# Zero products on TensorE near the start, and projection operands at half a 64-byte line

## The chip, the cores and the metric

The kernel runs on one core of a Trainium2 chip. The metric is the device time of one execution in microseconds. Before the change it is 289.07 us, the median of 3 runs (288.51 to 289.23).

## The reference

Inputs are float32. Attention has 2 batches, 8 heads, 768 positions and 64 elements a head; a query sees the first 8 keys and the 96 keys that end at itself, with a linear bias by distance and head. Its output goes through two gated networks. What is computed, cut to what matters:

```
scores = q @ k.T / sqrt(64) - slope[h] * dist         # outside the window: -1e9
x  = (softmax(scores) @ v) as [2, 768, 512]
g1 = sigmoid(causal depthwise conv of x, 5 taps)
x  = (g1 * (x @ w_val)) @ w_out                       # 512 -> 512 -> 512
h  = relu(x @ w_in)                                   # 512 -> 1024
g2 = sigmoid(depthwise conv of h, 3 taps)
out = (h * g2) @ w_out2                               # 1024 -> 512
```

## The kernel before, in words

A tile is 128 partitions high. Attention works on 12 tiles of 128 queries (2 batches of 6). For each, PE makes the scores against this tile's keys and those of the tile before (`scores`, L461), DVE adds the bias and takes the maximum (`least`, L472), ACT takes the exponential (L477), DVE divides by the sum (L498), PE transposes (L522) and multiplies with the values (L540). These products are plain f32; each leaves two records in the trace. The keys of tile 0 are loaded ahead of all else into a part of `c.x` that is still free (L835, L836); tile 1 is the first that uses keys loaded in the main part (`load`, L434).

The weights come as 64-bit floats and are turned into f32 by ACT, POOL and DVE (`to_f32`, L252). `w_out` and `w_in` are multiplied with each other once (`weights`, L319, f32, into two banks called f), so that the two layers between the gates are one. Every operand of the later products is split in a high and a low part of type fp32r (`split_ops`), and a product is three matmuls (`mm3`, L243 to L245): high by high, high by low, low by high. The 768 positions go in two chunks of 400 and 368 columns a batch, four in all. For each chunk `values` multiplies with `w_val` (moving operand `gx`), `hidden` with the joined weights `Wh`, `Wl` (moving operand `gg`), DVE convolves and gates, and `project` multiplies the result `g2` (loaded as stationary operand) with `w_out2` (moving operand, 512 columns, called wo2 here and lying in four tiles named w8). In the last chunk, the last of its three groups of rows is split into two halves of 256 columns, and the very last half goes out by DVE (L802) and a DMA.

SBUF tiles lie in pools one behind the other, in steps of 32 bytes: `const` (x, ident, Wh, Wl, wv), `w8`, `wst` (raw, m: staging of weights), `sg` (z, gx, gg, h, z2), and then `at` (attention's tiles) or, when attention is done, `late` (g2, o) in the same place; `small` lies at the other end. In the kernel before, every pool begins on a 64-byte line; inside `at`, the tile `st` of 96 bytes in three buffers leaves v and pts at half a line, and inside `sg` every second h tile is at half a line. PSUM has eight banks: four s, one t, one x, two f.

The order of the work around the change: the first part of the program is written out by hand (L833 to L845): DMAs, position and mask tiles, and the load of two numbers into registers of each engine (`values_load_multi_w_load_instructions`, L841), on which a branch between two forms of the kernel hangs (L938). All the rest is laid out by a planner (`Plan`): each piece of work has an engine, a cost in microseconds, the buffers that it holds and the names that it reads and writes; the planner lays the pieces on a model of the engines, and the order so found is the order in which each engine gets its instructions. A piece with `mode="s"` is drawn to others of its mode on PE.

Of the kernel before, what the change touches and what calls it, by code (L numbers as in the profile page):

```python
# [9 lines left out]
F32 = mybir.dt.float32  # L10
# [5 lines left out]
PSUM = bass.MemoryType.PSUM  # L16

P = 128
# [208 lines left out]
def dma_us(kb):  # L227
    return max(0.4, kb / 385.0)
# [118 lines left out]
        parts_unit(c, c.w_out2, a, lambda z, a=a, two=two: two[z].t[:, a % 4, :], two, ("wo2", a))  # L347


def scratch(c):  # L350

    x = [c.x[:, d, XP:] for d in range(NC1)]
    c.rel, c.w, c.d = (x[d][:, 0:WIN] for d in range(3))
    c.key, c.far, c.d0 = (x[d][:, 4 * P : 5 * P] for d in range(3))


def positions(c):

    nc = c.nc
    nc.gpsimd.iota(c.rel, pattern=[[-1, WIN]], base=P, channel_multiplier=1, allow_small_or_imprecise_dtypes=True)  # L360
    nc.gpsimd.iota(c.key, pattern=[[1, P]], base=0, channel_multiplier=0, allow_small_or_imprecise_dtypes=True)
    nc.gpsimd.affine_select(
        out=c.rel, in_=c.rel, compare_op=ALU.is_ge, fill=BIG, base=P, pattern=[[-1, WIN]], channel_multiplier=1
    )


def first_mask(c):

    nc = c.nc
    lf = c.small.tile([P, 2], F32, name="lf")  # L370
    nc.vector.tensor_copy(lf, c.li[:, :, 0])
    c.ng, c.nl = ng, nl = lf[:, 0:1], lf[:, 1:2]
    rel, w = c.rel[:, P:], c.w[:, P:]
    nc.vector.tensor_scalar(c.far, c.key, ng, BIG, ALU.is_ge, ALU.mult)
    nc.vector.scalar_tensor_tensor(w, rel, nl, c.far, ALU.is_ge, ALU.mult)
    nc.vector.scalar_tensor_tensor(c.d0, rel, nl, w, ALU.min, ALU.add)
# [32 lines left out]
def fast_attention(c, ap):  # L409

    nc, ident, pl = c.nc, c.ident, c.plan
# [9 lines left out]
    kq, vs = {}, {}  # L421
# [7 lines left out]
    def load(t):  # L429
        b, i = tiles[t]  # L430
        if t == 0:
            return
        kq[t], vs[t] = kqr.new(), vr.new()
        pl.add("SP", dma_us(512), lambda: nc.sync.dma_start(kq[t].t, c.kq[b, i]), [kq[t]], [], [("kq", t)], delay=LANDING)  # L434
        src = c.v[b, i * P : (i + 1) * P].rearrange("s h d -> s (h d)")
        pl.add(
            "SP", dma_us(256), lambda: nc.sync.dma_start(vs[t].t.rearrange("p a h d -> p (a h d)"), src),
            [vs[t]], [], [("v", t)], delay=LANDING,
        )

    def held(d, ts):
        return [d[t] for t in ts if t in d]

    for t in range(nt):
# [3 lines left out]
        js = [t - 1, t] if i else [t]  # L448
        nk = len(js) * P
        st, p = sts.new(), {}  # L450
        load(t)
        for half in range(2):
            s = [c.ring["s"].new() for z in range(2)]

            def scores(half=half, s=s, js=js, t0=t):
# [5 lines left out]
                            nc.tensor.matmul(out, keys(t0, pr, 1)[hs], keys(j, pr, 0)[hs], start=True, stop=True)  # L461

            pl.add(
                "PE", 0.43 * len(js), scores, s + held(kq, js), [("kq", j) for j in js], [("s", t, half)], mode="s"
            )
            for h in range(4 * half, 4 * half + 4):
                p[h] = pr_.new()
# [345 lines left out]
def attention_gated_mlps(ctx, tc, kq, v, nn, w_val, conv_w, w_out, w_in2, w_out2, out):  # L813
    nc = tc.nc
    c = Ctx()
# [4 lines left out]
    c.const = ctx.enter_context(tc.tile_pool(name="const", bufs=1))  # L820
    w8 = ctx.enter_context(tc.tile_pool(name="w8", bufs=1))
    c.wst = ctx.enter_context(tc.tile_pool(name="wst", bufs=1))
    sg = ctx.enter_context(tc.tile_pool(name="sg", bufs=1))
    c.small = ctx.enter_context(tc.tile_pool(name="small", bufs=1, side="right"))
    c.x = c.const.tile([P, NC1, XW], F32, name="x")
# [7 lines left out]
    with tc.manual_schedule():  # L833
        nc.sync.dma_start(c.li.rearrange("p n t -> p (n t)"), c.nn.to_broadcast([P, 4]))
        nc.scalar.dma_start(k0[:, 0:2], kq[0, 0, :, 0:2])  # L835
        nc.sync.dma_start(k0[:, 2:4], kq[0, 0, :, 2:4])  # L836
        nc.scalar.dma_start(v0, v[0, 0:P].rearrange("s (a h) d -> s a h d", a=4))
        scratch(c)
        positions(c)
        nc.vector.memset(one, 0.0)  # L840
        _, (glo, ghi, llo, lhi) = nc.values_load_multi_w_load_instructions(c.nn)  # L841
        nc.scalar.activation(one, one, AF.Exp)
        nc.gpsimd.memset(c.x[:, :, 0:XP], 0.0)
        make_identity(nc, c.ident)
        first_mask(c)  # L845
# [9 lines left out]
    def arm(fast):  # L855
        with ExitStack() as es:
# [4 lines left out]
            pl = c.plan = Plan()  # L861
            ap = pools.enter_context(tc.tile_pool(name="at", bufs=1)) if fast else None
            late = {}

            def late_pool():
                if not late:
                    pools.close()
                    late["p"] = pools.enter_context(tc.tile_pool(name="late", bufs=1, reuse_waits="tile"))
                return late["p"]

            def all_keys(b):
# [16 lines left out]
            c.ring["h"] = sb(here, "h", [P, CW + 2], F32, HBUFS)  # L888
            c.ring["z2"] = sb(here, "z2", [P, CH], F32, Z2BUFS)
            c.ring["g2"] = sb(late_pool, "g2", [P, 2, CH], F32R, 8)  # L890
            c.ring["o"] = sb(late_pool, "o", [P, DM], F32, 2)
            c.raws = sb(lambda: c.wst, "raw", [P, 512, 2], I32, RAWS)
            c.ms = sb(lambda: c.wst, "m", [P, 512], F32, MBUFS)
# [5 lines left out]
            if fast:  # L899
                masks(c, ap)  # L900
                attention = fast_attention(c, ap)
                next(attention)
                n0 = len(pl.work)
# [78 lines left out]
```

## Time and profile before

| | |
|---|---|
| median of 3 runs | 289.07 us |
| profiled execution | 288.96 us |
| its span | 287.2 us |
| PE busy | 269.2 us (94%), 1832 instructions |
| DVE busy | 238.6 us (83%) |
| ACT busy | 192.6 us (67%) |
| POOL busy | 68.5 us (24%) |
| HBM read, written | 22.59 MB, 3.15 MB |

The span runs from the first to the last instruction of the profiled execution. PE is the matmul engine (TensorE), PEld its loads of stationary operands, DVE VectorE, ACT ScalarE, POOL GpSimd, SPq the queue that issues most DMAs. Busy time is that in which an engine has an instruction under way; matmuls overlap each other, so that the duration of one is more than the time between two starts. `s<-w,g` are the projection's matmuls, `f<-gg,Wh` and the like the hidden layer's, `s<-kq` the attention's scores.

### The profile page before, as it was taken

The page shows a single profiled execution, that of the slowest core. Times are in us where ns is not written, and L with a number is a line of the kernel's source. Part 1 is how long each engine was busy: PE and PEld are TensorE (multiplying, and loading weights), DVE is VectorE, ACT ScalarE, POOL GpSimd, SP SyncE. Part 2 cuts the span into 40 slices and gives each one's busy share as a digit, 9 for nine tenths or more (in the row PEclk, how much of TensorE's full clock was granted, in tenths as well). Part 3 has the DMA queues.
Part 4 walks back from the last instruction along what each step waited for, and adds up shares of the span by engine and source line. Part 5 has one row for each costly group of instructions (what it writes and reads, how often), then busy time and mean ns, then how long its engine had stood idle before and what let it go on. Part 6 is the DMA issues. An engine that isn't in the chain of part 4 may idle for free.

```text
span 287.2 us, 5402 instructions
## 1 busy us (share of the span) xinstructions
PE 269.2 (94%) x1832; PEld 228.0 (79%) x1832; DVE 238.6 (83%) x637; ACT 192.6 (67%) x486; POOL 68.5 (24%) x160
## 2 busy tenths in 40 slices
PE   2687899899999999999999999999999999999993
PEld 2565666565447999999999999988999988899882
DVE  3999999999999999999899999999986654357600
ACT  2899998988568989988778544875355354454510
POOL 4422223522111120212353512360612000003000
PEclk9999999999999999999999999999999999999999
DMA  4984668637406301004510000010000011000112
GB/s 132 362 312 168 188 216 266 237 102 266 149 2 219 102 19 49 10 2 155 181 40 0 2 0 1 1 39 37 38 2 0 0 73 39 37 0 2 40 73 84
DMA packets 10277, 26.18 MB, mean 91 GB/s; under 512 B 1408, under 2 KB 2688, under 8 KB 10240
## 3 DMA queue, kind: packets, MB, share of 16 engines
q1 hardware_dynamic: 9440, 25.22, 26.3%
q10 hardware_dynamic: 800, 0.52, 0.6%
q8 instruction: 16, 0.26, 0.4%
q14 instruction: 21, 0.17, 0.2%
HBM read 22.59 MB, written 3.15 MB: 90 GB/s over the span
## 4 chain that ended last, share of the span: by engine, by line
PE 72%; DVE 20%; issue 3%; DMA 2%; ACT 1%; POOL 1%; SPq 0%; DVEq 0%; POOLq 0%
PE s L244 8%; PE s L245 8%; PE s L243 8%; PE f L243 7%; PE f L245 7%; PE f L244 7%; DVE p L472 5%; DVE p L498 4%; PE s L461 4%; PE x L540 4%; PE t L522 4%; DVE raw L269 3%; PE t L243 2%; PE x L245 2%; PE t L245 2%
## 5 line engine op out<-in xcount | busy, mean ns | idle before, releaser
L652 DVE SCALAR_TENSOR_TENSOR z<-h,cw,z 128x384 f32<-128x384 f32 x64 | 40.6, 643 | 12.6 <-ACT z L647 10.9
L477 ACT ACTIVATE p<-p,st 128x256 f32<-128x256 f32 (+1 forms) x96 | 46.0, 482 | 5.8 <-DVE st L472 5.5
L654 ACT ACTIVATE z<-z 128x384 f32<-128x384 f32 (+2 forms) x48 | 25.0, 523 | 26.7 <-DVE z L652 26.4
L244 PE MATMUL s<-w,g 128*128 128x512 f32 (+1 forms) x104 | 39.2, 377 | 0.0
L245 PE MATMUL s<-w,g 128*128 128x512 f32 (+1 forms) x104 | 39.2, 377 | 0.0
L243 PE MATMUL s<-w,g 128*128 128x512 f32 (+1 forms) x104 | 39.1, 376 | 0.0
L652 DVE SCALAR_TENSOR_TENSOR z<-x,cw,z 128x400 f32<-128x400 f32 (+1 forms) x64 | 38.4, 628 | 0.1
L522 PE MATMUL t<-ident,p 128*128 128x128 f32 x176 | 28.6, 281 | 4.7 <-ACT pts L526 4.7
L498 DVE TENSOR_SCALAR p<-p,st 128x256 f32<-128x256 f32 (+1 forms) x96 | 31.1, 368 | 0.7
L522 PEld LDWEIGHTS t<-ident,p 128*128 128x128 f32 x176 | 19.9, 140 | 14.6 <-ACT pts L526 8.5
L472 DVE CUSTOM_DVE_ANT_0 p<-s,B 128x256 f32<-128x256 f32 x80 | 30.7, 417 | 0.4 <-PE t L522 0.4
L319 PE MATMUL f<-w,w 128*128 128x512 f32 x64 | 30.1, 601 | 0.7 <-DVE Wl L236 0.6
L526 ACT ACTIVATE pts<-t 128x512 f32<-128x512 f32 (+1 forms) x48 | 26.5, 553 | 2.5 <-PE t L522 2.1
L243 PE MATMUL f<-gg,Wh 128*128 128x400 f32 (+1 forms) x80 | 27.7, 346 | 0.0
L245 PE MATMUL f<-gg,Wl 128*128 128x400 f32 (+1 forms) x80 | 27.0, 338 | 0.0
L244 PE MATMUL f<-gg,Wh 128*128 128x400 f32 (+1 forms) x80 | 27.0, 338 | 0.0
L461 PE MATMUL s<-kq 64*128 64x128 f32 x320 | 25.0, 291 | 0.5 <-DVE st L472 0.5
L461 PEld LDWEIGHTS s<-kq 64*128 64x128 f32 x320 | 21.0, 194 | 5.5 <-issue 3.2
L264 POOL TENSOR_SCALAR raw<-raw 128x512 f32<-128x512 f32 x24 | 17.7, 739 | 27.2 <-ACT m L262 21.6
L648 POOL TENSOR_SCALAR z<-h,cw 128x384 f32<-128x384 f32 x12 | 11.4, 947 | 49.1 <-DVE z L652 31.0
L245 PEld LDWEIGHTS s<-w,g 128*128 128x128 f32 x104 | 19.5, 188 | 3.8
L236 DVE TENSOR_TENSOR g<-z,g 128x384 fp32r<-128x384 f32 x32 | 17.4, 550 | 5.9 <-ACT g L234 5.9
(114 smaller groups left out, 606.4 us busy)
## 6 DMA issues: line engine op xcount, KB each, us to landing
raw<-in_moe_w_out_dram SPq DMA_DIRECT2D x12, 512.0 KB, 3.4
kq<-in_kq_dram SPq DMA_DIRECT2D x11, 512.0 KB, 5.1
raw<-in_moe_w_in_dram SPq DMA_DIRECT2D x8, 512.0 KB, 4.4
v<-in_v_dram SPq DMA_DIRECT2D x11, 256.0 KB, 3.9
out_dram<-o SPq DMA_DIRECT2D x11, 256.0 KB, 2.0
raw<-in_moe_w_val_dram SPq DMA_DIRECT2D x4, 512.0 KB, 4.0
v<-in_v_dram SPq DMA_DIRECT2D x8, 64.0 KB, 2.7
x<-in_kq_dram ACTq DMA_DIRECT2D x1, 256.0 KB, 4.1
```

Of the source, the lines that this page charges most:

```text
L243: nc.tensor.matmul(out, lh, rh, start=first, stop=False)
L244: nc.tensor.matmul(out, lh, rl, start=False, stop=False)
L245: nc.tensor.matmul(out, ll, rh, start=False, stop=last)
L319: nc.tensor.matmul(ps.t, big["wot"].t.bitcast(F32)[:, e, cs], big[wi].t.bitcast(F32)[:, e, :], start=e == 0, stop=e == 3)
L461: nc.tensor.matmul(out, keys(t0, pr, 1)[hs], keys(j, pr, 0)[hs], start=True, stop=True)
L472: nc.vector.tensor_tensor_reduce(w.t[:, :nk], sc, bias, -QKSCALE, 3.0e38, ALU.add, ALU.min, st.t[:, 0, h : h + 1])
L477: nc.scalar.activation(w.t[:, :nk], w.t[:, :nk], AF.Exp, bias=st.t[:, 0, h : h + 1], scale=-1.0, accum_out=st.t[:, 1, h : h + 1],)
L498: nc.vector.tensor_scalar(w.t[:, :nk], w.t[:, :nk], st.t[:, 2, h : h + 1], None, ALU.mult)
L522: nc.tensor.transpose(o[:, z, n, :], p[2 * pr + z].t[:, n * P : (n + 1) * P], ident)
L526: nc.scalar.activation(w.t[:, :, :nw, :], o[:, :, :nw, :], AF.Copy)
L652: nc.vector.scalar_tensor_tensor(z(), src(k), w()[:, k : k + 1], z(), ALU.mult, ALU.add)
L654: pl.add("ACT", act_us(n), lambda: nc.scalar.activation(z(), z(), AF.Tanh, scale=0.5), bufs, [], [token])
```

## The change

It does three things. A new function `idle` issues f32 products of zeros, with both operands read from one constant. Three of them, of 512, 512 and 256 columns, stand ahead of the register load in a PSUM pool of their own, closed at once. Two more, of 512 columns, are a piece of planned work on PE with cost 1.72 us and one f bank; it reads the names of tile 0's scores, and tile 1's scores read its name, so that it stands between them. Last, an unused tile of 32 bytes is put at the head of the pools `w8`, `wst` and `late`.

```diff
--- before.py
+++ after.py
@@ -347,6 +347,13 @@
         parts_unit(c, c.w_out2, a, lambda z, a=a, two=two: two[z].t[:, a % 4, :], two, ("wo2", a))
 
 
+def idle(c, out, widths):
+
+    for n in widths:
+        zeros = [c.nc.const_aps.tensor(0.0, [P, w], F32) for w in (P, n)]
+        c.nc.tensor.matmul(out[:, :n], *zeros, start=True, stop=True)
+
+
 def scratch(c):
 
     x = [c.x[:, d, XP:] for d in range(NC1)]
@@ -449,6 +456,9 @@
         nk = len(js) * P
         st, p = sts.new(), {}
         load(t)
+        if t == 1:
+            rest = c.ring["f"].new()
+            pl.add("PE", 1.72, lambda rest=rest: idle(c, rest.t, [512, 512]), [rest], [("s", 0, half) for half in range(2)], ["idle"])
         for half in range(2):
             s = [c.ring["s"].new() for z in range(2)]
 
@@ -461,7 +471,7 @@
                             nc.tensor.matmul(out, keys(t0, pr, 1)[hs], keys(j, pr, 0)[hs], start=True, stop=True)
 
             pl.add(
-                "PE", 0.43 * len(js), scores, s + held(kq, js), [("kq", j) for j in js], [("s", t, half)], mode="s"
+                "PE", 0.43 * len(js), scores, s + held(kq, js), [("kq", j) for j in js] + ["idle"] * (t == 1), [("s", t, half)], mode="s"
             )
             for h in range(4 * half, 4 * half + 4):
                 p[h] = pr_.new()
@@ -820,6 +830,8 @@
     c.const = ctx.enter_context(tc.tile_pool(name="const", bufs=1))
     w8 = ctx.enter_context(tc.tile_pool(name="w8", bufs=1))
     c.wst = ctx.enter_context(tc.tile_pool(name="wst", bufs=1))
+    for pool in (w8, c.wst):
+        pool.tile([P, 8], F32, name="half_line")
     sg = ctx.enter_context(tc.tile_pool(name="sg", bufs=1))
     c.small = ctx.enter_context(tc.tile_pool(name="small", bufs=1, side="right"))
     c.x = c.const.tile([P, NC1, XW], F32, name="x")
@@ -835,6 +847,8 @@
         nc.scalar.dma_start(k0[:, 0:2], kq[0, 0, :, 0:2])
         nc.sync.dma_start(k0[:, 2:4], kq[0, 0, :, 2:4])
         nc.scalar.dma_start(v0, v[0, 0:P].rearrange("s (a h) d -> s a h d", a=4))
+        with tc.tile_pool(name="pw", bufs=1, space=PSUM) as pw:
+            idle(c, pw.tile([P, 512], F32, name="idle"), [512, 512, 256])
         scratch(c)
         positions(c)
         nc.vector.memset(one, 0.0)
@@ -866,6 +880,7 @@
                 if not late:
                     pools.close()
                     late["p"] = pools.enter_context(tc.tile_pool(name="late", bufs=1, reuse_waits="tile"))
+                    late["p"].tile([P, 8], F32, name="half_line")
                 return late["p"]
 
             def all_keys(b):
```

## Rows read from the trace of the kernel before

**Rows 1.** the page, busy us, share of the span and instructions of each engine
```profile
PE 269.2 (94%) x1832; PEld 228.0 (79%) x1832; DVE 238.6 (83%) x637; ACT 192.6 (67%) x486; POOL 68.5 (24%) x160
```

**Rows 2.** stages: from:to, length, busy us of each engine, PEclk, DMA share, GB/s
```profile
0.00:4.90 4.90, 0.00 (x0) 0.00 (x0) 0.58 (x4) 0.23 (x1) 1.34 (x9) 1.00 0.39 125
...
9.05:12.87 3.82, 3.79 (x33) 3.59 (x34) 3.75 (x20) 3.26 (x13) 1.62 (x5) 1.00 1.03 370
12.87:30.00 17.13, 13.95 (x158) 10.68 (x159) 16.23 (x66) 16.23 (x53) 4.94 (x12) 1.00 0.69 242
30.00:80.75 50.75, 48.57 (x364) 30.32 (x364) 50.00 (x166) 43.09 (x127) 15.48 (x28) 1.00 0.62 197
...
142.80:282.70 139.90, 139.42 (x734) 127.43 (x732) 104.68 (x193) 74.65 (x151) 30.04 (x66) 1.00 0.07 25
```

**Rows 3.** chain of waits: start us, us, what
```profile
9.10 3.77 PE s L461 x32
```

**Rows 4.** timeline: start us, us, engine, line, tiles, count [idle before, releaser]
```profile
0.81 0.06 DVE L840 MEMSET one<- 128x1 f32 x1 [0.81 <-PEq L956]
...
4.97 2.08 PE L461 MATMUL s<-x 64*128 64x128 f32 x16 [4.97 <-DMA x<-in_kq_dram]
...
6.03 0.72 DVE L385 TENSOR_SCALAR b<-x 128x128 f32<-128x128 f32 x3 [0.45 <-DVE x L376]
...
6.66 0.28 DVE L472 CUSTOM_DVE_ANT_0 p<-s,b 128x128 f32<-128x128 f32 x1
...
9.08 0.80 PE L461 MATMUL s<-x,kq 64*128 64x128 f32 x4 [2.03 <-DVE x L401]
...
11.59 0.42 DVE L472 CUSTOM_DVE_ANT_0 p<-s,B 128x256 f32<-128x256 f32 x1
...
13.28 0.42 DVE L472 CUSTOM_DVE_ANT_0 p<-s,B 128x256 f32<-128x256 f32 x1 [0.38 <-PE t L522]
...
14.08 1.16 PE L461 MATMUL s<-kq 64*128 64x128 f32 x16
```

**Rows 5.** groups by line and form, PE: count, busy us, mean ns, idle
```profile
L244 PE MATMUL s<-w,g 128*128 128x512 f32 x88 | 34.8, 396 | 0.0
...
L319 PE MATMUL f<-w,w 128*128 128x512 f32 x64 | 30.1, 601 | 0.7 <-DVE Wl L236 0.6
...
L243 PE MATMUL f<-gg,Wh 128*128 128x368 f32 x32 | 10.6, 331 | 0.0
L244 PE MATMUL f<-gg,Wh 128*128 128x368 f32 x32 | 10.5, 329 | 0.0
...
L244 PE MATMUL s<-w,g 128*128 128x256 f32 x16 | 4.4, 276 | 0.0
...
L461 PE MATMUL s<-x 64*128 64x128 f32 x16 | 2.1, 435 | 5.0 <-DMA x<-in_kq_dram 5.0
```

**Rows 6.** timeline of PE, ten records of L319
```profile
69.70 4.46 PE L319 MATMUL f<-w,w 128*128 128x512 f32 x10
```

**Rows 7.** the projection's matmuls alone in their stretch, busy us of PE
```profile
142.80:282.70 139.90, 71.30 (x312) 1.00 0.07 25
```

**Rows 8.** timeline of PE: projection, then hidden layer, from start to start
```profile
250.46 0.39 PE L243 MATMUL s<-w,g 128*128 128x512 f32 x1
250.69 0.39 PE L244 MATMUL s<-w,g 128*128 128x512 f32 x1
...
251.16 0.39 PE L243 MATMUL s<-w,g 128*128 128x512 f32 x1
...
253.25 0.33 PE L243 MATMUL x<-gg,Wh 128*128 128x368 f32 x1
...
255.27 0.33 PE L243 MATMUL f<-gg,Wh 128*128 128x368 f32 x1
```

**Rows 9.** timeline of PE, the attention's products L540
```profile
129.00 1.97 PE L540 MATMUL x<-pts,v 128*64 128x128 f32 x32
```

**Rows 10.** line L652 on DVE: duration ns min/median/max, first and last start
```profile
L652 DVE SCALAR_TENSOR_TENSOR z<-h,cw,z x64: 601/617/999, 125.4 to 269.8; 128x384 f32<-128x384 f32 x64
```

## The prediction

> **What bounds the kernel now.** I read the busy times first [rows 1]: PE 94%, DVE 83%. A mean over stages says little, so the stages come next [rows 2]. There the reader sees three kernels in one. Until 9.05 us everything waits for loads and masks. From there to 80.75 us DVE is the full engine (3.75 of 3.82 us, 50.00 of 50.75). From 142.8 to 282.7 us it is PE (139.42 of 139.90), while DVE has room (104.68). Third, the chain of waits [rows 3] gives the order: in its early part PE's scores of the second tile, 3.77 us from 9.10, between stretches of DVE; later PE all along, and at the end DVE's last copy and the output's DMA. Fourth, the timeline tells PE's pace inside the stages, from start to start, since the duration of one matmul is a latency that overlaps the next.
>
> **The register load and the first zeros.** The first scores start at 4.97 and sixteen records take 2.08 us; at 14.08 sixteen of the same size take 1.16 us [rows 4], the second group being of another tile. So PE runs at 1.2 GHz at first and at 2.4 GHz by 14.08, although the windows print a granted clock of 1.00 from the start [rows 2]. After the first scores PE idles 2.03 us and then works from 9.08, still slowly.
>
> The change puts three f32 products of 512, 512 and 256 columns ahead of the register load. Price: an f32 product leaves two records (L319's 32 products leave 64 [rows 5]); ten such records take 4.46 us, the last of them 0.60, so (4.46 - 0.60)/9 = 0.43 us each at 2.4 GHz [rows 6]. 512 columns are 0.86 us, 1280 columns 2.15 us, and at half clock 4.3 us. PE has nothing else until 4.9 us (x0 in rows 2). Starting near 0.8 us, where DVE starts its first instruction [rows 4], the zeros end near 5.1 us, 0.1 us after the scores' present start. Cover: DVE makes masks from 6.03 to 6.75 and reads its first scores at 6.66 [rows 4]; the first half of the scores, (2.08 - 0.43)/2 after their start and a latency of 0.43 [rows 5], is there at 6.2, or 6.3 with the delay. So the delay costs nothing, and 0.1 us if that cover were gone. Behind the zeros on PE's queue stand the load of its registers and the branch. I take it that they are issued past the running zeros: 0. If they had to wait for the zeros' end, the scores would start up to 4.3 us later; no row shows either, and I keep that in the last rival.
>
> **The second zeros.** Two more products of 512 columns, 1.72 us at 2.4 GHz, stand between the first two tiles' scores. They start when the first scores end, near 7.1, and end by 8.9. The second tile's scores start at 9.08 [rows 4]. The view names DVE's L401 as what released them, but that reads none of their data; it is the tile's keys, by DMA, that they need, and the change moves no DMA. Hence 1.72 us in a gap of 2.03 us: nothing. They hold one of the two f banks, whose next user is L319, tens of microseconds later. Only the second tile's scores and what follows on PE stand behind them.
>
> **What the warm clock gives back.** The second tile's 32 records take 3.77 us [rows 3]; at the warm pace twice 1.16, at most 2.3 us, so up to 1.5 us less. But DVE does not wait for most of that: it works on old heads and masks and takes the first of these scores at 11.59 [rows 4], when half of them are done (9.08 + 1.9 = 11.0). What it waits is 0.38 us before 13.28 [rows 4]. Late next is DVE itself: from 12.87 to 30 us it is busy 16.23 of 17.13 [rows 2]. I take 0.4 us; the ends are a loss of 0.1 and a gain of 0.9 us, all of DVE's idle time there. After 30 us DVE is full to 80.75 and PE later, so 0.4 us stays 0.4 us at the end. The order of work comes from a planner, in whose model PE is free while the keys are on their way, so that I expect the same order; a tie that falls otherwise may move work, and I widen the range by 0.3 us each way for it.
>
> **The half lines.** By the layout of the program, all operands of the fast (fp32r) products begin on a 64-byte line. The pads move w8 by 32 bytes, wst, sg and the attention's pool by 64, late by 96: wo2 and g2, which the projection reads and loads, now begin half a line further, and all other operands of fast products stay on full lines. L319's operands lie in w8 too, but these are f32, at half speed. No instruction is added. The pads touch three lines of 88 products with 512 columns, 264, and three of 16 with 256, 48 [rows 5], 71.30 us of PE's work in the stretch where PE never waits [rows 7], so each nanosecond counts in full. Their pace: twelve start between 250.46 and 253.25, 232.5 ns each, where 512 columns at 2.4 GHz are 213.3; the next twelve, of 368 columns, take (255.27 - 253.25)/12 = 168.3 (153.3) [rows 8]. 512 columns take 396 ns from start to end and 256 take 276 [rows 5], 120 ns for 256 columns more, where the clock gives 106.7. The f32 records, which read half as fast, take 430 for 426.7. So the surplus is 19 ns at 512 columns, 15 at 368, some 6 at 256 and 3 at half speed: it grows with what is read and is there at full speed alone. That is what an operand's place in SBUF could touch. A shift by whole lines does not: gg's second half lies 25 lines behind its first, and L244, which reads it, takes 329 ns at 368 columns against 331 of L243 [rows 5].
>
> A half line at full speed does not occur in this trace. The nearest row is L540, whose pts and v lie at half lines now: 32 records in 1.97 us, so (1.97 - 0.27)/15 = 113 ns a pair, where the clock gives 106.7 [rows 9]; that is at half speed, and no penalty. Upper end: all surplus beyond 3 ns goes, 264 x 16 + 48 x 3 = 4.4 us. Lower end: one more stall in each. Starts lie 0.23 us apart and then (251.16 - 250.69)/2 = 0.235 [rows 8], which lets a step be about 5 ns; 312 x 5 = 1.6 us lost. L540 speaks neither for a loss nor for a gain at full speed. As the surplus is one of reading, and the change moves both operands of just these products, I take half of the upper end, 2.2 us. The vector engines write g2 and wo2 at the new places; every second h tile lies at a half line already (1608 bytes, laid 1632 apart), and L652 reads them in 601 ns at least and 617 in the middle [rows 10], with no second level, so I count nothing. If the projection goes faster, DVE's part is late next, which has a quarter of the stretch free.
>
> [...]
>
> **Sum.** The profiled execution took 288.96 us, 287.2 of span and 1.8 around it; the median of the runs, 289.07, is 0.1 above. 288.96 - 0.4 - 2.2 = 286.4, on the median 286.5.
>
> **Rivals.**
> - Half lines change nothing: the warm clock alone, 288.7. For it: no row shows an address to matter. Against: the surplus has no other cause in the rows, as PE waits for nobody there.
> - The whole surplus goes: 289.07 - 0.4 - 4.4 = 284.3. For it: at half speed products do run at the clock. Against: the place would have to be its only cause.
> - Half lines are worse: a read that begins in mid-line touches one line more, a stall of 5 ns in each of the 312 products; it decides from 0.4/312 = 1.3 ns on. 289.07 - 0.4 + 1.6 = 290.3. For it: 2048 bytes then touch 33 lines, not 32. Against: L540 shows no such toll.
> - The zeros come late: the clock is still low when the second pair runs, which then takes 3.4 us. From 7.2 it lasts to 10.6, the second tile starts 1.5 us later, and DVE's wait before 13.28 is 1.5 us longer: 290.6 with no gain from half lines. It decides when the zeros end after 9.08. Against: PE would then have been at work from 0.8 us on without a break, as it was from 9.08 before the rise that the trace shows.
>
> **Chances.** Forecast 0.40, whole surplus 0.13, nothing from half lines 0.29, worse 0.12, late zeros 0.06. A measurement of this kernel tells about 0.3%, 0.87 us, from no change. Faster: the first two, and 0.02 of the third, whose warm clock may give 0.9 us: 0.55. Same: the rest of the third and 0.01 of the fourth: 0.28. Slower: 0.17. The forecast's own range is 285.0 to 288.0; with the cases of both signs 283.8 to 290.0, which leaves out about 0.04 below and 0.13 above.
>
> **What would show it.** The sixteen first scores in 1.2 to 2.0 us instead of 2.08, the second tile's 32 in under 2.4 us from about 9.1, and DVE's wait before 13.28 gone. Twelve projecting products in 2.69 us (224 ns each) instead of 2.79, with 2.02 us for the hidden layer's twelve unchanged. A pace of still 232 is the first rival, 216 the second, 237 the third. The prediction is wrong if PE waits anywhere from 142.8 on, if another order of the work lets another engine end the early chain, or if the first scores start much after 5.1.

## The result, and the profile after

The changed kernel takes 291.77 us (median of 13 runs, 289.95 to 292.98), the one before 289.15 us (13 runs, 288.51 to 289.91). The ratio is 1.0072, 95% interval 1.005 to 1.0095: slower by 2.6 us by the medians and 2.1 us by the ratio, where 2.6 us less was forecast. The runs of the changed kernel fall in two groups: four of 289.95 to 290.13 us, with a mean granted clock of 0.994 to 0.998 (1 is full speed), and nine of 291.43 to 292.98 us, with 0.982 to 0.987. The profiled execution (291.43 us, span 289.7, 288.96 and 287.2 before) belongs to the second.

The page's busy times of the changed kernel, against [rows 1]:

```profile
PE 275.8 (95%) x1842; PEld 229.7 (79%) x1842; DVE 241.3 (83%) x638; ACT 191.1 (66%) x481; POOL 73.5 (25%) x164
```

PE's 6.6 us more are mostly the zeros (3.92 and 1.99 us), and cost nothing as such. DVE, which is full in the middle of the kernel (49.92 of 50.75 us), has 2.7 us more to do, and POOL 5.0 us more. The stages of the changed kernel, in the columns of [rows 2]:

```profile
9.05:12.87 3.82, 1.64 (x6) 0.94 (x8) 3.75 (x19) 2.60 (x11) 2.95 (x7) 0.71 0.96 322
12.87:30.00 17.13, 15.39 (x169) 12.62 (x168) 15.80 (x63) 14.46 (x47) 5.11 (x10) 0.86 0.77 269
30.00:80.75 50.75, 48.70 (x361) 29.73 (x361) 49.92 (x164) 42.25 (x125) 16.07 (x28) 1.00 0.58 189
...
142.80:282.70 139.90, 139.90 (x753) 127.79 (x753) 106.93 (x196) 78.98 (x159) 29.24 (x67) 1.00 0.08 28
```

PEclk, the third figure from the end of a row, is the share of its full clock that PE was granted. It says 0.71 and 0.86 where it said 1.00; of the 1.00 before, the first is only what is printed ahead of the record's first rise, at 12.81 there: until then sixteen records of the scores took 2.08 us, behind it 1.16 [rows 4]. In the changed kernel the record first rises at 3.85 us; ahead of that the zeros' records of 512 columns start 853 and 854 ns apart once the first has gone, those of the second group 431 and 433. Then it has a fall at 10.68 us and a rise at 17.51; windows cut there show it whole:

```profile
10.68:17.51 6.83, 6.28 (x44) 5.02 (x46) 5.74 (x25) 3.65 (x12) 2.89 (x6) 0.50 1.00 361
17.51:30.00 12.49, 10.76 (x133) 8.54 (x130) 12.22 (x48) 11.78 (x38) 3.70 (x7) 1.00 0.68 227
```

So the clock that the zeros were to warm is granted at 0.50 for 6.83 us. The timeline of PE tells what came before the fall (start us, us, line, tiles; L471 are the scores, L461 before; L532 the transposes, L522 before):

```profile
0.78 3.92 PE L354 MATMUL idle<-const-float32-0.0 128*128 128x512 f32 x6 [0.78 <-PEq L971]
5.30 1.16 PE L471 MATMUL s<-x 64*128 64x128 f32 x16 [0.61 <-DMA x<-in_kq_dram]
6.39 1.99 PE L354 MATMUL f<-const-float32-0.0 128*128 128x512 f32 x4
10.76 0.66 PE L532 MATMUL t<-ident,p 128*128 128x128 f32 x2 [2.38 <-DVE p L508]
11.90 0.69 PE L532 MATMUL t<-ident,p 128*128 128x128 f32 x2 [0.47 <-DVE st L501]
12.52 0.80 PE L471 MATMUL s<-x,kq 64*128 64x128 f32 x4
```

The first scores take 1.16 us instead of 2.08 (1.2 to 2.0 forecast) and the second zeros end at 8.38 (8.9 forecast). But what follows is another order: the transposes of tile 0 stand ahead of tile 1's scores, and wait 2.38 us for DVE's division (L508, L498 before), until 10.76. The scores that started at 9.08 [rows 4] start at 12.52, at a granted clock of 0.50, and in the chain of waits they take as long as ever [rows 3]:

```profile
12.59 3.72 PE s L471 x32
```

DVE's timeline shows that its wait on these scores has not gone but grown from 0.38 to 1.06 us (L482 is L472 before):

```profile
9.87 1.13 DVE L508 TENSOR_SCALAR p<-p,st 128x128 f32<-128x128 f32 x4
...
14.63 0.42 DVE L482 CUSTOM_DVE_ANT_0 p<-s,B 128x256 f32<-128x256 f32 x1 [1.06 <-PE s L471]
```

The same happens on SP's queue, where the first piece of `w_in` now stands ahead of tile 1's keys, which were issued at 5.41 before:

```profile
5.38 0.34 SPq L291 DMA_DIRECT2D raw<-in_moe_w_in_dram  x1
5.83 0.37 SPq L441 DMA_DIRECT2D kq<-in_kq_dram  x1
```

By the trace these keys land at 10.65 us instead of 8.95, so that tile 1's scores could not have started at 9.08 even without the transposes ahead of them. By the first product of the hidden layer most of the loss is there; that product in the trace before and after:

```profile
110.29 0.43 PE L243 MATMUL f<-gg,Wh 128*128 128x400 f32 x1
```

```profile
112.46 0.43 PE L243 MATMUL f<-gg,Wh 128*128 128x400 f32 x1
```

The first product of the projection starts at 151.26 instead of 148.93, the last at 284.54 instead of 281.94. So 2.2 of 2.6 us are lost ahead of the hidden layer.

The projection. The groups of PE by form, against [rows 5], and the starts of twelve hidden and twelve projecting products, against [rows 8]:

```profile
L244 PE MATMUL s<-w,g 128*128 128x512 f32 x88 | 34.7, 395 | 0.0
...
L244 PE MATMUL s<-w,g 128*128 128x256 f32 x16 | 4.5, 284 | 0.0
```

```profile
250.87 0.33 PE L243 MATMUL f<-gg,Wh 128*128 128x368 f32 x1
...
252.88 0.39 PE L243 MATMUL s<-w,g 128*128 128x512 f32 x1
...
255.66 0.33 PE L243 MATMUL x<-gg,Wh 128*128 128x368 f32 x1
```

(255.66 - 252.88)/12 = 231.7 ns, where it was 232.5: the half lines gave nothing at 512 columns. At 256 columns a product lasts 284 ns instead of 276.

Last, DVE's division of the large tiles (256 columns) by form, before and after:

```profile
L498 DVE TENSOR_SCALAR p<-p,st 128x256 f32<-128x256 f32 x80 | 26.1, 370 | 0.5
```

```profile
L508 DVE TENSOR_SCALAR p<-p,st 128x256 f32<-128x256 f32 x80 | 28.7, 397 | 0.6
```

The number of instructions is the same; they take 2.6 us longer. That is nearly all that DVE has more.

### The profile page after: what moved, and what is told of

Read it like the earlier page. It is cut to its first block, busy times and chain, and to the rows that moved or that the text cites. A ratio compares the mean times of both kernels' runs of the same rounds, so it can differ in the third digit from the quotient of the medians.

```text
span 289.7 us, 5431 instructions
## 1 busy us (share of the span) xinstructions
PE 275.8 (95%) x1842; PEld 229.7 (79%) x1842; DVE 241.3 (83%) x638; ACT 191.1 (66%) x481; POOL 73.5 (25%) x164
## 4 chain that ended last, share of the span: by engine, by line
PE 63%; DVE 26%; ACT 5%; issue 3%; POOL 1%; DVEq 1%; POOLq 0%; ACTq 0%
PE s L244 8%; PE s L245 8%; PE s L243 8%; DVE p L508 6%; PE f L243 6%; PE f L244 6%; PE f L245 6%; DVE z L662 5%; DVE p L482 5%; PE s L471 4%; PE x L550 3%; ACT p L487 3%; PE t L532 3%; PE t L243 2%; PE t L245 2%
## 5 line engine op out<-in xcount | busy, mean ns | idle before, releaser
L243 PE MATMUL s<-w,g 128*128 128x512 f32 (+1 forms) x104 | 39.2, 377 | 0.0
L245 PE MATMUL s<-w,g 128*128 128x512 f32 (+1 forms) x104 | 39.2, 377 | 0.0
L662 DVE SCALAR_TENSOR_TENSOR z<-x,cw,z 128x400 f32<-128x400 f32 (+1 forms) x64 | 37.8, 634 | 0.0
L532 PE MATMUL t<-ident,p 128*128 128x128 f32 x176 | 29.5, 287 | 6.6 <-ACT pts L536 2.8
L532 PEld LDWEIGHTS t<-ident,p 128*128 128x128 f32 x176 | 19.9, 142 | 19.8 <-ACT pts L536 12.2
L508 DVE TENSOR_SCALAR p<-p,st 128x256 f32<-128x256 f32 (+1 forms) x96 | 33.2, 387 | 0.8
L482 DVE CUSTOM_DVE_ANT_0 p<-s,B 128x256 f32<-128x256 f32 x80 | 30.3, 415 | 1.1 <-PE s L471 1.1
L319 PE MATMUL f<-w,w 128*128 128x512 f32 x64 | 31.0, 601 | 0.0
L243 PE MATMUL f<-gg,Wh 128*128 128x400 f32 (+1 forms) x80 | 27.6, 345 | 0.0
L245 PE MATMUL f<-gg,Wl 128*128 128x400 f32 (+1 forms) x80 | 27.1, 338 | 0.0
L264 POOL TENSOR_SCALAR raw<-raw 128x512 f32<-128x512 f32 x24 | 17.9, 751 | 31.7 <-ACT m L262 20.9
L471 PEld LDWEIGHTS s<-kq 64*128 64x128 f32 x320 | 21.0, 194 | 5.7 <-issue 3.6
L471 PE MATMUL s<-kq 64*128 64x128 f32 x320 | 24.9, 291 | 0.1
L236 DVE TENSOR_TENSOR g<-z,g 128x384 fp32r<-128x384 f32 x32 | 18.0, 568 | 5.9 <-ACT g L234 5.9
L234 ACT ACTIVATE g<-z 128x384 fp32r<-128x384 f32 x32 | 16.5, 522 | 9.6 <-DVE z L775 8.0
L245 PEld LDWEIGHTS s<-w,g 128*128 128x128 f32 x104 | 19.6, 188 | 3.9
```

What stands on the lines that cost most here:

```text
L243: nc.tensor.matmul(out, lh, rh, start=first, stop=False)
L245: nc.tensor.matmul(out, ll, rh, start=False, stop=last)
L319: nc.tensor.matmul(ps.t, big["wot"].t.bitcast(F32)[:, e, cs], big[wi].t.bitcast(F32)[:, e, :], start=e == 0, stop=e == 3)
L482: nc.vector.tensor_tensor_reduce(w.t[:, :nk], sc, bias, -QKSCALE, 3.0e38, ALU.add, ALU.min, st.t[:, 0, h : h + 1])
L508: nc.vector.tensor_scalar(w.t[:, :nk], w.t[:, :nk], st.t[:, 2, h : h + 1], None, ALU.mult)
L532: nc.tensor.transpose(o[:, z, n, :], p[2 * pr + z].t[:, n * P : (n + 1) * P], ident)
```

## Experiments

**One part each.** First the three unused tiles alone, on the kernel before; no zeros, and the order of before.

```diff
+    for pool in (w8, c.wst):
+        pool.tile([P, 8], F32, name="half_line")
...
+                    late["p"].tile([P, 8], F32, name="half_line")
```

> The pads alone on the kernel before, whose order of instructions stays the same on every engine. Theory (the planner's new order and the clock cost the time, the half lines next to nothing): between 0 and +0.3 us against before, pace of the 512-column products 232 ns as before, that of the 256-column products perhaps 120 instead of 113 ns. Rival 1 (half lines cost the time): +1.5 to +2.6 us. Rival 2 (half lines gain 2.2 us, as forecast, and something else eats it): 2.2 us faster, 224 ns.

289.47 us, ratio 1.0006 (0.9989 to 1.0022), as expected. PE's projection alone; its groups by form are those of the changed kernel, 395 and 284 ns:

```profile
142.80:282.70 139.90, 71.23 (x312) 55.13 (x312) 0.00 (x0) 6.54 (x12) 1.00 0.07 26
```

71.23 us against 71.30 [rows 7]: no gain, and no loss that the time shows. The 48 products of 256 columns go from 114 ns up to 120 from start to start (means of 42 pairs of neighbours), 0.3 us in all.

Next the order alone: the changed kernel without pads and first zeros, whose planned piece issues nothing.

```diff
-            pl.add("PE", 1.72, lambda rest=rest: idle(c, rest.t, [512, 512]), [rest], ...
+            pl.add("PE", 1.72, lambda rest=rest: None, [rest], ...
```

> The planned piece of 1.72 us stays, so the order is that of the changed kernel, but it issues nothing; no first zeros, no pads. Theory: the order alone makes it slower, by 0.9 us at least (what the changed kernel loses in its quicker group of runs) and up to 2.7 us, since PE is then at 1.2 GHz in the whole early part. Rival (the zeros themselves cost the time): within 0.3 us of before.

292.43 us, ratio 1.0093 (1.0068 to 1.0119): a loss of 2.7 us, the upper end of what was expected, with nothing added but a piece of work in the plan. Without zeros PE is slow until 17.65 us here (four records of the scores start 0.43 us apart, as under a granted clock of 0.50), so that this loss need not be made up like that of the changed kernel. Its timeline of PE:

```profile
4.92 2.08 PE L471 MATMUL s<-x 64*128 64x128 f32 x16 [4.92 <-DMA x<-in_kq_dram]
10.48 0.66 PE L532 MATMUL t<-ident,p 128*128 128x128 f32 x2 [3.48 <-DVE p L508]
...
12.23 0.80 PE L471 MATMUL s<-x,kq 64*128 64x128 f32 x4
```

The new order comes from the plan. The planner lays the work six times, each time with ranks from the time before, and keeps the lay that ends first in its own model. Before, that was the second (268.03 in the model's us); with the piece in the list all six change, and the fourth wins with 267.52. The same new order comes out for costs of the piece of 0, 0.1, 0.43, 0.86, 1.29 and 1.72 us: its presence changes the ranks, not its length. The model gives the new order half a microsecond less, the chip 2.6 us more.

Then both groups of zeros without a new order, and without pads: the second group is issued by the piece that makes tile 0's scores.

```diff
                             nc.tensor.matmul(out, keys(t0, pr, 1)[hs], keys(j, pr, 0)[hs], start=True, stop=True)
+                if (t0, half) == (0, 1):
+                    idle(c, c.psum.tile([P, 512], F32, tag="f", name="f"), [512, 512])
```

> Both groups of zeros on the kernel before, the second issued inside the piece that makes the second half of tile 0's scores, so that the planner sees no new piece and the order on PE, DVE, ACT and POOL stays that of before; no pads. Theory: the clock stays up from about 4 us, tile 1's scores take 2.0 to 2.3 us from 9.1 on, DVE's wait before 13.3 goes: 0.3 to 0.9 us faster than before, all runs within 0.5 us. Rival (the zeros cost the time): 0.9 us slower or more, and two groups of runs.

288.55 us, ratio 0.9967 (0.9948 to 0.9985), 0.95 us less than before by the ratio, 0.7 by the medians. The runs spread over 1.7 us, not 0.5 as expected. PE's timeline:

```profile
0.78 4.61 PE L354 MATMUL idle<-const-float32-0.0 128*128 128x512 f32 x6 [0.78 <-PEq L967]
5.49 1.17 PE L468 MATMUL s<-x 64*128 64x128 f32 x16
6.58 1.99 PE L354 MATMUL f<-const-float32-0.0 128*128 128x512 f32 x4
9.25 0.49 PE L468 MATMUL s<-x,kq 64*128 64x128 f32 x4 [0.67 <-DVE x L408]
```

Tile 1's scores start where they did, at a granted clock of 1.00 to the end, and DVE's wait of 0.38 us is gone. This is the zeros' part as the prediction described it, and a version faster than both kernels.

The first zeros alone, on the order of before:

```diff
+        with tc.tile_pool(name="pw", bufs=1, space=PSUM) as pw:
+            idle(c, pw.tile([P, 512], F32, name="idle"), [512, 512, 256])
```

> Only the first zeros, ahead of the register load, on the kernel before; order of all else as before. Theory (what helps is a clock that is up for tile 1's scores): the clock rises near 4 to 5.5 us, tile 0's scores take 1.2 to 1.6 us, then PE idles 2.5 us until tile 1's scores; they run partly or wholly at full clock: between 0.2 and 0.9 us faster than before, with more spread than with the second zeros. Rival (the second zeros do the work by holding the clock): within 0.2 us of before.

288.74 us, ratio 0.999 (0.9974 to 1.0006): 0.3 us less, with an interval that holds both expectations and overlaps that of the run with both groups, so that the times don't show what the second group is worth. The windows show why it is there:

```profile
6.04:9.46 3.42, 1.46 (x25) 1.29 (x24) 3.38 (x24) 2.55 (x14) 1.69 (x6) 1.00 0.85 314
9.46:12.87 3.41, 3.29 (x29) 2.67 (x25) 3.34 (x16) 2.89 (x11) 1.96 (x6) 0.50 1.02 350
```

After a stretch in which PE was busy 1.46 of 3.42 us the clock falls to 0.50, just under tile 1's scores, which start at 8.86.

**Does a longer second group help?** The changed kernel with five products in the planned piece instead of two, the new order unchanged.

```diff
-idle(c, rest.t, [512, 512])
+idle(c, rest.t, [512] * 5)
```

> The changed kernel with five products of 512 columns in the second group of zeros instead of two, planned at the same cost, so in the same order: they last to about 10.7 us and close PE's idle stretch. Theory (the two groups of runs differ by the granted clock, which falls after that stretch): one group only, near 290.0 us, mean granted clock 0.99 or more in all. Rival (the groups have another cause): two groups of about 290.0 and 291.8 as in the changed kernel; or the longer zeros delay tile 0's transposes and all runs are slower than 291.

291.22 us, ratio 1.0062 (1.0042 to 1.0082). One group of runs (290.82 to 291.59), as expected: the zeros fill PE's gap up to 10.97 and no run has a mean clock under 0.992. But the level is not that of the changed kernel's quick group; it stands 1.2 us above it. Part of that may be the clock after all: five of the six runs have a mean clock of 0.992 or 0.993, and 0.993 is what the last run below has in its profiled execution, with one fall of 3.4 us. The sixth, the profiled one, has 0.998 and no fall ahead of 287.97 us, and takes 290.82 us, 0.7 above the quick group; that I can't explain. So a warm clock at the start is not enough.

**The surplus of the fast products.** If it were a toll per instruction or a limit of long reads, halves would show it. On the kernel before, the projection's products of 512 columns are issued as two of 256, except the first and the last of each group.

```diff
-            mm3(nc, po[n].t[:, :w], g2[f].t[:, 0, ts], ..., f == 0, f == NC2 - 1)
+            lh, ll = (g2[f].t[:, z, ts] for z in range(2))
+            for m, (l, r) in enumerate(((lh, wh), (lh, wl), (ll, wh))):
+                first, last = f == m == 0, f == NC2 - 1 and m == 2
+                for o in range(0, w, w if first or last else DM // 2):
+                    e = w if first or last else o + DM // 2
+                    nc.tensor.matmul(po[n].t[:, o:e], l, r[:, f % 4, c0 + o : c0 + e], start=first, stop=last)
```

> No zeros and no pads: the kernel before, with each projecting product of 512 columns but the first and the last of a group issued as two of 256 columns with the same stationary operand, 22 of 24 in each group. Theory (the surplus of a fast product comes with the length of one read, 19 ns at 512 columns and 6 at 256): a pair takes 226 ns instead of 232.5, so 264 x 22/24 x 6.5 = 1.6 us faster, 287.7. Rival 1 (the short products' pace of 113 ns in the trace of before belongs to the quiet end of the kernel): 232 ns a pair or more, no change. Rival 2 (a second load of the stationary operand costs): slower, some 240 ns a pair, +1.8 us.

289.53 us, ratio 1.0002 (0.9984 to 1.0021). Over 490 pairs of neighbouring starts a half takes 115.7 ns, so 231.4 for two, as much as one product of 512. The expected gain is not there. With it the pace is known at four widths, in ns a column: 115.7/256 = 0.452 at 256 columns, 180.8/400 = 0.452 at 400, 168/368 = 0.457 at 368, 232.5/512 = 0.454 at 512. The time, and the surplus in it, goes with the columns and not with the number of instructions.

The same halves on top of the zeros in the old order:

> Both zeros in the old order (as in the run with the old order) and the projection in halves of 256 columns. Theory (both gains stand in different stages, DVE's and PE's, and add): 0.9 + 1.6 = 2.5 us faster than before, 286.7. Rival (DVE's part of the projection becomes late): no more than 1.6 us faster.

288.28 us, ratio 0.9967 (0.9949 to 0.9986): the zeros' gain, and nothing from the halves.

**The changed kernel again**, with nothing edited, for its groups of runs:

> The changed kernel once more, beside the others. Theory: +0.7% against before, runs in two groups near 290.0 and 291.8, the quick group with a mean granted clock of 0.994 or more. If its trace is of the quick group, the clock's fall between 10.7 and 17.5 us is missing or shorter in it and tile 1's scores take 1.9 to 2.3 us; DVE is still slower than before in L498, L269 and L652 by 10 to 40 ns an instruction, as POOL works beside it. Rival (the quick group has another order of events, such as earlier loads): the clock falls as in the first trace.

290.42 us, ratio 1.0053 (1.003 to 1.0076); five of ten runs lie at 289.96 to 290.19 us, the others from 290.64 to 292.25. The mean clock is a rough sign only: one of the five has 0.990, and runs of the old order with zeros go down to 0.989 (289.87 us in the third experiment). In its profiled run (291.94) the clock fell twice:

```profile
12.91:16.32 3.41, 3.41 (x28) 2.53 (x26) 3.41 (x15) 2.50 (x9) 0.97 (x3) 0.50 1.01 370
...
23.15:26.56 3.41, 3.41 (x28) 2.85 (x28) 3.29 (x13) 2.73 (x9) 1.14 (x2) 0.50 0.69 215
```

**The whole change on the order of before**: the zeros as in the third experiment, with the three unused tiles of the first.

> The whole change without a new order: both groups of zeros (the second inside the piece that makes the first tile's scores) and the three unused tiles, on the order of before. My theory: the half lines give nothing and cost at most 0.3 us in the 48 products of 256 columns, the zeros give their 0.4 to 1 us, so 288.2 to 289.0 us and a pace of 232 ns for 512 columns. Rival, the prediction as it stood: with the order kept, the half lines do pay, and the time is 286.5 us, the pace 224 ns. Second rival: zeros and unused tiles together cost something that neither does alone, and the time is 290 us or more with the order of before.

288.75 us, ratio 0.9986 (0.9967 to 1.0006). The projection alone:

```profile
142.80:282.70 139.90, 71.46 (x312) 55.14 (x312) 0.42 (x1) 6.92 (x12) 1.00 0.07 24
```

So the forecast's 286.5 us fails even with the order kept: 71.46 us against 71.30 [rows 7]. What the zeros gain stays, about 0.4 us with the tiles and 0.95 without; the two intervals overlap.

**Start or rest of the order?** The changed kernel, in whose list tile 1's keys go ahead of the first piece of `w_in` again, and tile 0's transposes, with all that hangs on them, behind tile 1's scores. The rest of the new order is left.

```diff
+        first = next(w for w in order if w.eng == "SP")
+        keys = self.tag["kq", 1]
+        if first is not keys:
+            order.remove(keys)
+            order.insert(order.index(first), keys)
+        last = order.index(self.tag["s", 1, 1])
+        held = set(self.tag["t", 0, pr] for pr in range(NPAIR))
+        for w in order[:last]:
+            if w.pred & held:
+                held.add(w)
...
+        return kept + moved + order[last + 1:]
```

> The changed kernel with its new order but for the start: the second tile's keys are again loaded ahead of the first piece of w_in, and the second tile's scores stand again ahead of the first tile's transposes; the rest of the new order on all engines is left. My theory: what costs is this exchange at the start (2.38 us in which PE waits for DVE, the clock that falls, and DVE's waits after it), so 288.5 to 289.6 us, with the second tile's scores from 9.1 us and the clock at full speed to the end. Rival: the later order costs (more of the conversions on POOL, at the side of which DVE is slower), and the exchange at the start is made up elsewhere: 290.5 to 291.8 us though the scores come at 9.1 us. Between 289.6 and 290.5 both would hold.

292.1 us, ratio 1.0078 (1.004 to 1.0116), in two groups: six runs of 290.06 to 290.67, six of 293.53 to 294.27. My theory (288.5 to 289.6 us) fell. The scores come early:

```profile
9.17 0.49 PE L491 MATMUL s<-x,kq 64*128 64x128 f32 x4 [0.85 <-DVE st L502]
...
15.19 1.19 PE L491 MATMUL s<-kq 64*128 64x128 f32 x6 [1.15 <-DVE st L502]
```

and the quick runs stand where the changed kernel's stand, 290.06 us; by these runs the exchange at the start cost them nothing. And the clock still falls, in the profiled run (293.53) twice, after 14.54 and after 24.78:

```profile
14.54:21.37 6.83, 6.18 (x43) 5.10 (x44) 5.88 (x27) 5.09 (x18) 1.87 (x5) 0.50 0.85 329
...
24.78:28.20 3.42, 3.42 (x26) 2.87 (x28) 2.76 (x10) 2.61 (x8) 1.12 (x2) 0.50 0.36 132
```

So two things are to be explained: 1.5 us without a fall (the runs of clock 0.996 and more: median 290.07 here, 288.57 in the run before), and the falls. For the first the groups of DVE show where to look, the division again, here and then in the whole change on the order of before (L528 and L507 are the same line):

```profile
L528 DVE TENSOR_SCALAR p<-p,st 128x256 f32<-128x256 f32 x80 | 29.5, 407 | 0.6
```

```profile
L507 DVE TENSOR_SCALAR p<-p,st 128x256 f32<-128x256 f32 x80 | 25.5, 363 | 0.5
```

A median division takes some 347 ns in both. In these two traces the long ones all run beside POOL, at work on a conversion (L264, here L283) or a filter. One such meeting, first POOL, then DVE:

```profile
50.54 0.84 POOL L283 TENSOR_SCALAR raw<-raw 128x512 f32<-128x512 f32 x1 [2.44 <-ACT w L281]
```

```profile
50.75 0.78 DVE L528 TENSOR_SCALAR p<-p,st 128x256 f32<-128x256 f32 x1
```

The old order has 4 divisions of over 390 ns, the new one 13, of up to 815. The count varies from run to run: the other traces of the old order have 5 to 8 (the kernel before 6), those of the new one 11 to 14.

So the long divisions are those beside POOL. What holds them up there, and whether they stand still to POOL's very end, is not shown here, as POOL's spans are rough; nor is every division beside POOL long (335 to 386 ns for 34 of 51 in the traces of the kernel before and the changed one).

**Take POOL away.** The last two runs, with POOL's step of each conversion cut from 512 columns to 8, in both orders. They leave out most of POOL's share of the conversions, so that the weights they work with are not the reference's.

```diff
-nc.gpsimd.tensor_scalar(whole(), whole(), 0.0, ...
+nc.gpsimd.tensor_scalar(whole()[..., :8], whole()[..., :8], 0.0, ...
```

> The whole change on the order of before, with POOL's step of each conversion (L264) cut from 512 columns to 8 (of each of the four pieces where there are four), so that it leaves out most of POOL's work there; order and waits stay. My theory: DVE's division (L498, 256 columns) takes 347 ns alone and about 680 beside POOL's L264, and the old order has 4 such meetings, the new one 13 up to 140 us. With POOL's step short the old order gains some 1 us (288.75 to about 287.7) and its longest division stays below 450 ns. Rival: meetings on the same engine time don't set the end; the time stays at 288.3 to 289.0.

> The new order with its start put back, and POOL's step of the conversions (L264) cut to 8 columns as in the run beside it. Before that, and in the runs whose clock didn't fall, the new order took 290.06 and the old 288.75 us: 1.3 us more. My theory: the 9 more meetings of DVE's divisions with POOL cost that, so the new order now gains 2 to 3.5 us in the runs whose clock doesn't fall, and stands within 0.5 us of the old order's run beside it. Rival: the new order is longer by what it does on the other engines or in PE's order, and stays 1 to 1.6 us above the old order's run. The falls of the clock, 3.6 us in 5 of 12 runs, should stay in both cases, as nothing at the start is touched.

Old order: 287.18 us, ratio 0.9924 (0.99 to 0.9948). New order: 289.11 us, ratio 1.0 (0.9971 to 1.0028). DVE's division in the one, then in the other:

```profile
L507 DVE TENSOR_SCALAR p<-p,st 128x256 f32<-128x256 f32 x80 | 24.5, 351 | 0.5
```

```profile
L528 DVE TENSOR_SCALAR p<-p,st 128x256 f32<-128x256 f32 x80 | 25.4, 356 | 0.6
```

In the runs of clock 0.996 and more the old order takes 287.17 us (five runs), the new one 287.44 (two runs): 0.3 us apart instead of 1.5. The new order gains 2.6 us, the old one 1.4. That bears the theory out, with few runs on one side. It doesn't part the meetings from the rest of what POOL's step does: a shorter one also ends sooner for what waits for it, and in the profiled run before the cut (293.53 us, new order) DVE waits 2.3 us for L283 itself. Against that rival stands the one kept trace of the new order without a fall, that of the longer second group. It has no such wait. Up to the first product of the hidden layer (111.06 us there, 109.72 in the whole change on the order of before) DVE, the third engine of a row, is busy 2.1 us more and idle 0.8 us less:

```profile
0.00:111.06 111.06, 104.62 (x841) 71.88 (x841) 104.91 (x360) 87.72 (x258) 35.23 (x75) 1.00 0.56 185
```

```profile
0.00:109.72 109.72, 100.95 (x834) 70.18 (x835) 102.80 (x361) 89.56 (x263) 31.13 (x70) 1.00 0.56 182
```

The falls stayed as expected: six runs of the new order have a mean clock of 0.992 or 0.993 (288.43 to 289.58 us) and four 0.981 to 0.986 (290.10 to 291.07). In the profiled one (mean clock 0.993) the clock fell late, from 88.63 to 92.04 us, after PE had waited 1.87 us for POOL. Products with `w_val` (fp32r, 400 columns; L262 to L264 are L243 to L245 before) run in that stretch:

```profile
89.85 0.54 PE L263 MATMUL f<-gx,wvh 128*128 128x400 f32 x1
...
91.51 0.54 PE L262 MATMUL f<-gx,wvh 128*128 128x400 f32 x1
```

Five steps in 1.66 us are 332 ns each, at a granted clock of 0.50. Half of that is 166 ns, but at full clock 400 columns take 180.8: twice the clock doesn't halve the time, and the difference, 15 ns, is the surplus.

**The account.** From 289.15 us: the zeros and the unused tiles in the order of before, 0.9986, give 0.4 us back; the new order costs 1.5 us in runs of like clock, for the most part through POOL's work beside DVE (0.3 us are left when that is cut), which makes 290.2, the level of the four quick runs (289.95 to 290.13); the nine others, whose low mean clock speaks of falls, stand 1.8 us higher (median 291.85) and set the median of all.

## Why the prediction was wrong

- **The step that failed:** "The order of work comes from a planner, in whose model PE is free while the keys are on their way, so that I expect the same order". The order changed on every engine, and the order alone costs 2.7 us. The 0.3 us by which I widened the range for it was a tenth of that. "The change moves no DMA" fell with it: SP's queue changed too, and tile 1's keys land 1.7 us later. That the scores wait for these keys, and not for DVE's L401, was read rightly: with the order kept they start 0.13 us behind the landing (8.95 and 9.08 before, 9.04 and 9.17 in the whole change on the order of before).
- **The second step that failed: the half lines, "I take half of the upper end, 2.2 us".** This term measured nothing, at most 0.3 us lost in the 256-column products, and without it the forecast fails with the order kept too (288.75 us). The first rival was right on this part. The surplus was read rightly, 19 ns at 512 columns, more the more is read: 332 ns for 400 columns at a granted clock of 0.50 (the last run) are 1.2 columns a ns, the prediction's 1.2 GHz; from that and twice the clock I estimate 212.5 ns at 512 columns (213.3 in the prediction) and 166 at 400, where 232.5 and 180.8 were measured. The f32 records go from 853.5 ns to 429.5, 3 ns above the half. That an address could touch the surplus was only argued, and the line of 64 bytes is a way of counting addresses: no run shows that SBUF is read in such lines. The shift of wo2 by 32 bytes and of g2 by 96 left the products of 512 columns as they were (232.5 and 231.7 ns) and made those of 256 longer (114.2 and 119.9).
- **The zeros:** right in price and place. They start at 0.78 and end at 4.70 (5.1 predicted), or at 5.39 in the third experiment, where they took 4.61 us instead of 3.92. The registers' load and the branch behind them don't wait for their end: in that experiment's trace the branch is over at 4.75 us, as before (4.76), and the scores start at 5.49, behind the zeros. In the changed kernel's own trace the load itself lasts until 4.29 us instead of 3.91, the branch until 5.14, and the scores start at 5.30; the view names a DMA there that had landed at 4.80. DVE reads its first scores at 6.89 there and at 6.71 in the third experiment, instead of 6.66. The second group takes 1.99 us from 6.39. The 0.4 us of the warm clock stand, once the order is kept: 0.95 us with the interval 0.4 to 1.5. DVE's wait that is gone explains 0.38 of it; where the rest comes from no run shows.
- **The rivals:** the one that ended at 290.6, late zeros and a low clock under tile 1's scores, had the right place and sign, but the wrong cause: the zeros were in time, PE waited for DVE and for the keys afterwards.
- **A sign of being wrong, "if another order of the work lets another engine end the early chain",** named the case; I gave it no chance of its own, though with the new piece in the list all six lays of the planner came out otherwise.

Open are two points. What makes the clock fall in some runs of the new order and not in others of the same kernel isn't settled: it is not the exchange at the start alone, since the run that undid this had the falls. In the kept traces falls stand behind waits of PE: one of 2.38 us ahead of the fall at 10.68, one of 1.77 us ahead of that at 12.91, one of 1.87 us ahead of that at 88.63. But the whole change on the order of before has a wait of 1.45 us, to 13.05, and no fall, so that the waits alone don't tell which runs fall. And the longer second group should have reached the quick runs' 290.1 us; its one run that surely had no fall took 290.82.

## What to carry to other kernels

Where a program lays out the order, adding a planned piece, however short, can be adding a new order: compare the two orders on every engine before pricing the piece, or issue the new work from within a piece that is already there, which here turned 2.6 us lost into 0.4 us gained (0.95 without the unused tiles). A surplus in a row is not yet a saving: price what the edit is known to remove, and let one part run alone before it carries most of the sum. When runs of one kernel fall into groups, set the mean granted clock beside each time, and compare orders only between runs of like clock.

## What the runs showed of the hardware

- Products of type fp32r take 0.452 to 0.457 ns a column at a granted clock of 1.00, at 256, 368, 400 and 512 columns alike; two of 256 cost as much as one of 512 (231.4 and 232.5 ns). At a granted clock of 0.50 400 columns take 332 ns (the last run), 1.84 times the 180.8 at full clock and not twice.
- Moving wo2 by 32 bytes and g2 by 96 left products of 512 columns alone (232.5 and 231.7 ns) and slowed 256 columns by some 6 ns each (114.2 and 119.9).
- A division of 256 columns on DVE took 333 to 365 ns when POOL had nothing under way (medians 347.5 in the kernel before, 349 in the changed one). Beside POOL 34 of 51 took 335 to 386 ns; the 17 longer ones, 436 to 822, all ran beside a conversion or a filter. The instruction that reads scores from PSUM (L472) has medians of 417 ns with POOL beside it and 417 without in the kernel before, 417 and 414 in the changed one.
- The granted clock fell again to 0.50 for 3.4 or 6.8 us well after the start, at 9.46, 10.68, 12.91, 14.54, 23.15, 24.48, 24.78 and once at 88.63 us; four records of the scores take 0.43 us from start to start there instead of 0.22.
- PE's branch behind products that still ran wasn't held up by them: it was over at 4.75 us while the first zeros ran to 5.39 (third experiment).
